# Two equal units a batch in the first stage of a fused attention and two-layer MLP kernel, and loads that gather across unit borders

## The chip, the cores and the metric

The kernel runs on one core of a Trainium2 chip. The metric is the device time of one launch in microseconds (us). Engines are named as in the profile: PE is the matrix engine (PEld its weight loads), DVE the vector engine, ACT the scalar engine, POOL GpSimd, SP the queue that issues every DMA of this kernel (SPq in the rows).

## What is computed

The reference, cut to what matters (B = 8 batches, H = 8 heads, S = 576 tokens, D = 64; 4608 tokens in all, d_model 512, d_ff 2048):

```
a = softmax(phi over 32 slots)
k_m, v_m = einsum('bhsm,bhsd->bhmd', a, k), the same with v
attn = softmax(q @ k_m^T / 8) @ v_m
x = attn, heads side by side: 4608 x 512
r = relu(x @ moe_w_in);  g = s * r * r + b
y = g @ moe_w_out
h = y @ moe2_w_in;  out = (h * sigmoid(1.702 h)) @ moe2_w_out
```

Every product of float32 matrices is made of three matmuls of a high part and a low part (fp32r): high by high, high by low, low by high.

## The kernel before

The program has four stages, one after the other on PE:

- **Stage 1** goes over the 8 batches of 576 tokens. For a batch, `slots` and `attend` make the attention weights of the tokens, 32 slots a head, transposed, and `weigh` leaves them as a high part `ah` and a low part `al` (two head groups, 576 columns each). `matrix` folds v_m into a quarter of moe_w_in on PE (tile `vw`), and ACT and DVE split that into `mh` and `ml`. `step` then makes 256 rows of `h = x @ moe_w_in` for one unit of tokens: 12 matmuls (2 row blocks, 2 head groups, 3 parts) whose moving operand is the unit's columns of `ah` or `al`. ACT (or DVE) takes relu of it into a tile `r`, and a DMA writes that to DRAM. A batch has 8 values of `pi` (256 rows each), and for each of these two units.
- **Stage 2** (`down("wo", "r", ...)`) goes over 6 spans of 768 tokens, each two half blocks of TS = 384 tokens. It loads `r` from DRAM as [128, 2, 384] tiles, five a span and quarter (A, B, C, D, E: 120 loads in all), squares them on ACT (line 642), combines and splits them on DVE and ACT (`ol`, `oh`) and makes seven products of a Strassen scheme; `leave` writes tiles `x`.
- **Stage 3** (`up`) reads `x` and writes `g`; **stage 4** (`down("w2", "g", ...)`) reads `g` and writes the output.

Since 576 is not a multiple of 384, the units of stage 1 are cut at the borders of the 384-token half blocks. `units(b)` yields them: 384 and 192 tokens for an even batch, 192 and 384 for an odd one. A unit of 384 tokens then fills one DRAM tile `r` of [128, 2 x 384] by itself; a unit of 192 tokens fills half of one, as 2 runs a partition of 192 values. `attend` and `weigh` make the attention columns in the same units; in batch 0 the two units are weighed one after the other, in the later batches together.

The order of the work is found at build time by `Order.sort`: each operation has a due time, a cost for each engine that can do it, and needs; the planner takes, engine by engine, what can start first, and writes the program in that order. `pe` costs a group of `count` matmuls of n columns as count x (n / 2.4 + 13.4) ns; `dma` and the loads cost kb / 340 us on SP. The due times of stage 1 go by B1 = 38.5 us a batch, and loads of stage 2 are due 14 to 16 us ahead of their product. Buffers come from pools of fixed numbers (`BUFS`): 31 of the tiles `t`, 4 of PSUM. In the start, until batch 0 is under way, PE runs filler matmuls of 128 columns (line 228) in front of a PSUM tile's first use.

The matmuls of `step` stand in the trace at lines 280 to 282 (helper `mm3`), their relu at line 598, the casts of every operand at line 258, the subtractions at line 264, stage 2's matmuls at lines 667 to 669, and every DMA at line 253.

Of the kernel before, what the change touches and what calls it, by code (L numbers as in the profile page):

```python
# [14 lines left out]
AF = mybir.ActivationFunctionType  # L15
ALU = mybir.AluOpType
# [136 lines left out]
class Net:  # L153
# [31 lines left out]
    B1, B2 = 38.5, 58.5  # L185
# [3 lines left out]
    def __init__(self, nc, tc, ctx, aps):  # L189
        self.nc, self.tc, self.a = nc, tc, aps  # L190
        self.B, self.S = aps["q"].shape[0], aps["q"].shape[3]
        self.sb = ctx.enter_context(tc.tile_pool(name="sb", bufs=1))
        self.ps = ctx.enter_context(tc.tile_pool(name="ps", bufs=1, space=PSUM))
        self.dr = ctx.enter_context(tc.tile_pool(name="dr", bufs=1, space=bass.MemoryType.DRAM))
        self.n = self.spare = 0
        self.T = {}
        self.order = Order(self.BUFS)
        self.d = {}
# [14 lines left out]

        return self.t(k, [P, 2, n], dt)

    def units(self, b):

        t = self.S * b
        while t < self.S * (b + 1):
            n = min(self.TS - t % self.TS, self.S * (b + 1) - t)  # L220
            m = t // self.TS
            yield t - self.S * b, n, m // 2, m % 2, t % self.TS
            t += n

    def pst(self, k):
# [261 lines left out]
    def attend(self, b, due, groups, apart):  # L487


        nc, T, S = self.nc, self.T, self.S  # L490
        at = [e[:2] for e in self.units(b)]
        qs = [("t", ("q", b, p)) for p in range(4)]
        kms = [("km", (b, g)) for g in range(2)]
        for p, k in enumerate(qs):
            self.dma(due - 8 + 0.5 * p, lambda k=k: self.t(k, [P, S]), lambda p=p: self.a["q"][b, p], (), (k,))
        for n, us in enumerate(groups):
            d = due + apart[1] * n
            ps = {u: ("ps", ("a", b, u)) for u in us}

            def score(us=us, ps=ps):  # L500
                for u in us:
                    out = self.pst(ps[u])
                    for p in range(4):
                        w = slice(32 * p, 32 * p + 32)
                        for g in range(2):
                            o = slice(64 * g, 64 * g + 64)
                            c, m = at[u]
                            nc.tensor.matmul(out[w, g, 0:m], T[kms[g]][o, w], T[qs[p]][o, c:c + m], start=True, stop=True)

            self.pe(d, 2200 * sum(at[u][1] for u in us) // S, score, (*qs, *kms), tuple(ps.values()))  # L510
            for g in range(2):
                self.weigh(b, g, us, [at[u] for u in us], ps, d, apart[0] * g)
# [65 lines left out]
        self.tt(due + 1, 1024, lambda: self.t(ml, [P, 2, 512], F32R), lambda: T[pm], lambda: T[mh].bitcast(F32), ALU.subtract, (pm, mh), (ml,))  # L578


    def step(self, b, pi, u, unit, due):
        nc, T = self.nc, self.T
        h, r = ("ps", ("h", b, pi, u)), ("t", ("r", b, pi, u))
        j = pi // 2
        c0, n, s, half, at = unit
        c = slice(c0, c0 + n)
        m = [("w", (x, b, j)) for x in ("mh", "ml")]
        ats = [[("t", (x, b, k)) for x in ("ah", "al")] for k in range(2)]

        def mm():  # L590
            out = self.pst(h)
            for i in range(2):
                o = slice((2 * pi + i) % 4 * P, (2 * pi + i) % 4 * P + P)
                self.mm3(out[:, i, 0:n], [([T[x][:, k, o] for x in m], [T[x][:, c] for x in ats[k]]) for k in range(2)])

        self.pe(due, n, mm, (*m, *((*x, u) for k in ats for x in k)), (h,), count=12)
        self.order.add(due + 0.5, [
            self.act(2 * n, lambda: nc.scalar.activation(self.two(r, n=n), T[h][:, :, 0:n], AF.Relu), psum=True),  # L598
            self.dve(2 * n, lambda: nc.vector.tensor_scalar(self.two(r, n=n), T[h][:, :, 0:n], 0.0, None, op0=ALU.max))], (h,), (r,))
        to = ("r", s, pi % 4, pi // 4, half)  # L600
        self.dma(due + 2, lambda: self.dram(*to).rearrange("p (a t) -> p a t", a=2)[:, :, at:at + n], lambda: T[r], (r,), ((*to, at),), n // 2)


    def operand(self, due, i, key, src, n):
# [10 lines left out]
        self.tt(due, 2 * self.TS, (lambda: self.two(out)) if new else (lambda: T[out]), lambda: T[a], lambda: T[b], ALU.subtract,  # L615
                [k for k in (a, b) if k != out], (out,))

    def load(self, due, k, name, *index):
        r = [x for x in self.order.wrote if x[:1 + len(index)] == (name, *index)]
        self.dma(due, lambda: self.two(k).rearrange("p a b -> p (a b)"), lambda: self.dram(name, *index), r, (k,), 384)  # L620

    def down(self, name, src, s, due):

# [107 lines left out]
    def up(self, s, due):  # L731

        nc, T, TS = self.nc, self.T, self.TS
        n = 2 * TS
        R = {(j, k): ("t", (f"x{j}{k}", s)) for j in range(2) for k in range(2)}
        for j, k in ((0, 0), (1, 0), (0, 1), (1, 1)):
            self.load(due - 26 + 2 * j + 4 * k, R[j, k], "x", s, j, k)
        r11, r12, r21, r22 = R[0, 0], R[0, 1], R[1, 0], R[1, 1]
        t2 = ("t", ("t2", s))
        op = {}  # L740
        d = due - 12
# [14 lines left out]
        for q in range(4):  # L756
            X, Y, Z = (("ps", (x, "w1", s, q)) for x in "XYZ")
            to = {1: X, 2: Z, 6: X, 7: Y, 5: X, 3: X, 4: Y}
            a, u2, u4 = (("t", (x, "w1", s, q)) for x in ("a", "u2", "u4"))
            for at, i in enumerate(seq):  # L760
                d = due + q * pair + at * pas
# [17 lines left out]
                e = d + pas  # L779
# [45 lines left out]
    def plan(self):  # L825
# [8 lines left out]
        for b in range(B):  # L834
            s0 = b * B1
            if b == 0:
                for g in range(2):
                    self.slots(0, g, -42 + 4 * g, 10)
                self.attend(0, -28, ((0,), (1,)), (2, 6))
            for j in range(4):  # L840
                if b == 0:
                    for c in range(4):
                        k = ("w", ("wi", j, c // 2))

                        def make(k=k, c=c):
                            if c % 2 == 0:
                                self.t(k, [P, 2, 512])
                            return self.T[k][:, c % 2]

                        self.convert(9.6 * j - 24 + 2 * c, (*k, c % 2), make, self.a["wi"][4 * j + c], 24 - 2 * c if j == 0 else 6)  # L850
                d = s0 + j * B1 / 4
                self.matrix(b, j, d - (24 if b == j == 0 else 8))
                if b == 0 and j == 2:
                    self.warm(d, False)
                for i in range(2):
                    for u, unit in enumerate(self.units(b)):
                        self.step(b, 2 * j + i, u, unit, d + B1 / 8 * (i + unit[0] / self.S))
                if b + 1 < B and j < 2:
                    self.slots(b + 1, j, s0 + 2 + 8 * j)
                elif b + 1 < B and j == 2:  # L860
                    self.attend(b + 1, s0 + 18, ((0, 1),), (4, 0))
            if b in (2, 3, 4, 6):
                q = (2, 3, 4, 6).index(b)
                self.prepare("wo", q, s0 + 2, keep=q == 3, step=3)
# [95 lines left out]
```

## Time and profile before

| | before |
|---|---|
| median of 3 runs | 1403.19 us (1402.94 to 1405.13) |
| the profiled execution's own time | 1407.16 us |
| its span in the profile | 1405.2 us |
| PE / DVE / ACT busy, share of the span | 98% / 74% / 57% |
| granted PE clock, mean | 0.995 |
| DMA moved | 347.74 MB, 247 GB/s over the span |

Busy time of PE counts a matmul from its start to its modelled end; successive matmuls overlap, so the distance from start to start, not the duration, is what one costs. In the rows, an entry such as "0.33 PE L281" is a duration, and the number at the row's start is the start time in us from the beginning of the span.

### The profile page before, as it was taken

The numbers are of one execution on the slowest core, as the hardware profiler recorded it, in microseconds if no ns is written. First come the engines' busy times: TensorE is split into PE (matmuls) and PEld (weight loads), VectorE is DVE, ScalarE is ACT, GpSimd is POOL, SyncE is SP. The second block draws the span as 40 slices with busy tenths as digits, with TensorE's granted clock in tenths as the row PEclk, the third lists the DMA queues.
The fourth block names the chain that finished last, engine by engine and source line by source line (L and its number), as shares of the span: only waits on it lengthen the run. The fifth ranks groups of instructions, "written<-read, shape, count | busy, mean of one in ns | idle before, by whom it ended". The sixth has DMA issues, their size and how long they took to land.

```text
span 1405.2 us, 23985 instructions
## 1 busy us (share of the span) xinstructions
PE 1381.0 (98%) x9250; PEld 1328.2 (95%) x9250; DVE 1041.4 (74%) x1411; ACT 795.8 (57%) x1113; POOL 92.0 (7%) x70
## 2 busy tenths in 40 slices
PE   7899999999999999999999999999999999999998
PEld 6788888789999999999999999999999999999998
DVE  6959898786698888988876756565356967869682
ACT  4456665576677787687745655554335434434341
POOL 1401110100100100000110110100000000000000
PEclk9999999999999999999999999999999999999999
DMA  9979999899875585499979674764896465344541
GB/s 349 305 255 302 378 368 332 291 311 358 280 246 187 182 277 173 153 320 320 337 261 345 259 271 166 257 238 147 277 360 242 155 195 177 125 158 162 195 138 45
DMA packets 134576, 347.74 MB, mean 247 GB/s; under 512 B 14400, under 2 KB 30784, under 8 KB 134464
## 3 DMA queue, kind: packets, MB, share of 16 engines
q1 hardware_dynamic: 134464, 346.24, 71.0%
q8 instruction: 72, 1.18, 0.3%
q14 instruction: 40, 0.33, 0.1%
HBM read 211.44 MB, written 134.74 MB: 246 GB/s over the span
## 4 chain that ended last, share of the span: by engine, by line
PE 85%; DMA 7%; DVE 6%; ACT 1%; issue 1%; SPq 1%; ACTq 0%; DVEq 0%
PE X L667 9%; PE X L669 9%; PE X L668 9%; PE Y L668 4%; PE Y L669 4%; PE Y L667 4%; PE X L774 4%; PE X L775 4%; PE X L776 4%; PE h L280 4%; PE h L282 4%; PE h L281 4%; PE Z L669 2%; PE Z L667 2%; PE Z L668 2%; DMA w<-w 2%
## 5 line engine op out<-in xcount | busy, mean ns | idle before, releaser
L282 PE MATMUL h<-ah,ml 128*128 128x384 f32 (+1 forms) x512 | 157.1, 307 | 5.5 <-DVE ml L264 5.5
L280 PE MATMUL h<-ah,mh 128*128 128x384 f32 (+1 forms) x512 | 161.0, 314 | 0.8 <-ACT km L258 0.5
L264 DVE TENSOR_TENSOR u<-Y,u 128x768 f32<-128x768 f32 x60 | 57.4, 956 | 135.5 <-ACT u L782 69.5
L281 PE MATMUL h<-al,mh 128*128 128x384 f32 (+1 forms) x512 | 156.6, 306 | 0.7 <-DVE al L264 0.7
L667 PE MATMUL X<-oh,wo 128*128 128x384 f32 x384 | 129.2, 337 | 2.9 <-ACT u L693 2.9
L774 PE MATMUL X<-oh,w 128*128 128x384 f32 x384 | 128.5, 335 | 1.1 <-ACT a L782 0.7
L668 PE MATMUL X<-ol,wo 128*128 128x384 f32 x384 | 129.0, 336 | 0.0
L669 PE MATMUL X<-oh,wo 128*128 128x384 f32 x384 | 128.8, 336 | 0.0
L776 PE MATMUL X<-oh,w 128*128 128x384 f32 x384 | 128.3, 334 | 0.0
L775 PE MATMUL X<-ol,w 128*128 128x384 f32 x384 | 128.3, 334 | 0.0
L667 PE MATMUL X<-oh,w 128*128 128x384 f32 x384 | 128.3, 334 | 0.0
L668 PE MATMUL X<-ol,w 128*128 128x384 f32 x384 | 128.3, 334 | 0.0
L669 PE MATMUL X<-oh,w 128*128 128x384 f32 x384 | 128.3, 334 | 0.0
L598 ACT ACTIVATE r<-h 128x768 f32<-128x768 f32 (+1 forms) x127 | 82.4, 651 | 67.6 <-PE h L282 54.9
L258 ACT CAST oh<-C 128x768 fp32r<-128x768 f32 x93 | 76.4, 835 | 67.2 <-PE X L669 26.0
L280 PEld LDWEIGHTS h<-ah,mh 128*128 128x128 f32 x512 | 97.8, 191 | 17.5 <-issue 6.3
L264 DVE TENSOR_TENSOR ol<-A,oh 128x768 fp32r<-128x768 f32 x96 | 91.9, 967 | 17.0 <-PE X L668 7.1
L282 PEld LDWEIGHTS h<-ah,ml 128*128 128x128 f32 x512 | 97.4, 190 | 6.6 <-DVE ml L264 6.6
L281 PEld LDWEIGHTS h<-al,mh 128*128 128x128 f32 x512 | 97.4, 190 | 1.6 <-DVE al L264 1.6
L264 DVE TENSOR_TENSOR ol<-C,oh 128x768 fp32r<-128x768 f32 x96 | 90.8, 956 | 8.1 <-ACT oh L258 4.0
L264 DVE TENSOR_TENSOR ol<-E,oh 128x768 fp32r<-128x768 f32 x48 | 45.8, 957 | 61.6 <-PE Y L668 21.4
L322 POOL TENSOR_TENSOR cw<-cw,raw 128x512 uint32<-128x512 uint32 x32 | 47.0, 1469 | 579.6 <-DVE cw L319 365.3
(192 smaller groups left out, 3725.7 us busy)
## 6 DMA issues: line engine op xcount, KB each, us to landing
w<-w SPq DMA_DIRECT2D x112, 512.0 KB, 5.6
r<-r SPq DMA_DIRECT2D x64, 384.0 KB, 5.2
wo<-wo SPq DMA_DIRECT2D x42, 512.0 KB, 6.0
g<-u SPq DMA_DIRECT2D x48, 384.0 KB, 3.2
kv<-in_kv SPq DMA_DIRECT2D x64, 258.0 KB, 5.3
raw<-in_w SPq DMA_DIRECT2D x32, 512.0 KB, 5.2
r<-r SPq DMA_DIRECT2D x64, 192.0 KB, 5.0
q<-in_q SPq DMA_DIRECT2D x32, 288.0 KB, 5.5
```

The source lines that it names most:

```text
L258: self.order.add(due, [self.act(n, lambda: nc.scalar.copy(out(), src()), psum), self.dve(n, lambda: nc.vector.tensor_copy(out(), src()), f ...
L264: self.order.add(due, [self.dve(n, lambda: nc.vector.tensor_tensor(out(), a(), b(), op=op), port=port)], r, w, first)
L280: self.nc.tensor.matmul(ps, wh, xh, start=start and i == 0, stop=False)
L281: self.nc.tensor.matmul(ps, wh, xl, start=False, stop=False)
L282: self.nc.tensor.matmul(ps, wl, xh, start=False, stop=(i == n - 1))
L598: self.act(2 * n, lambda: nc.scalar.activation(self.two(r, n=n), T[h][:, :, 0:n], AF.Relu), psum=True),
L667: nc.tensor.matmul(out, T[w][:, 0, c], T[h][:, p], start=f, stop=False, skip_group_check=True)
L668: nc.tensor.matmul(out, T[w][:, 0, c], T[l][:, p], start=False, stop=False, skip_group_check=True)
L669: nc.tensor.matmul(out, T[w][:, 1, c], T[h][:, p], start=False, stop=last, skip_group_check=True)
L774: nc.tensor.matmul(out, T[w][:, 0, c], T[h][:, k], start=f, stop=False, skip_group_check=True)
L775: nc.tensor.matmul(out, T[w][:, 0, c], T[l][:, k], start=False, stop=False, skip_group_check=True)
L776: nc.tensor.matmul(out, T[w][:, 1, c], T[h][:, k], start=False, stop=k == 1, skip_group_check=True)
```

## The change

Stage 1 works in two equal units of 288 tokens a batch (`HS = S // 2`), and the DRAM tiles of `r` are these units: one of [128, 2 x 288] for each batch, `pi` and unit, written by one DMA whose every partition is one run. `units` goes away; the new `pieces(m)` yields, for half block m of 384 tokens, the two units that it lies in, where in the unit and where in the tile, and how many tokens: 288 + 96, 192 + 192 or 96 + 288. `load` gathers an `r` tile of stage 2 by two DMAs from two DRAM tiles; loads of `x` and `g` stay one DMA each. `step` and `attend` take the fixed unit size; the due times of the two units are half a step apart, where they stood at 0 and two thirds, or 0 and a third.

```
+        self.HS = self.S // 2
-    def units(self, b):
-        t = self.S * b
-        while t < self.S * (b + 1):
-            n = min(self.TS - t % self.TS, self.S * (b + 1) - t)
-            m = t // self.TS
-            yield t - self.S * b, n, m // 2, m % 2, t % self.TS
+    def pieces(self, m):
+        t, end = self.TS * m, self.TS * (m + 1)
+        while t < end:
+            u, at = divmod(t, self.HS)
+            n = min(self.HS - at, end - t)
+            yield u // 2, u % 2, at, t - self.TS * m, n
             t += n
...
     def attend(self, b, due, groups, apart):
-        at = [e[:2] for e in self.units(b)]
+        at = [(0, self.HS), (self.HS, self.HS)]
...
-    def step(self, b, pi, u, unit, due):
+    def step(self, b, pi, u, due):
-        c0, n, s, half, at = unit
-        c = slice(c0, c0 + n)
+        c = slice(u * HS, u * HS + HS)
...
-        self.pe(due, n, mm, (*m, *((*x, u) for k in ats for x in k)), (h,), count=12)
+        self.pe(due, HS, mm, (*m, *((*x, u) for k in ats for x in k)), (h,), count=12)
...
-        to = ("r", s, pi % 4, pi // 4, half)
-        self.dma(due + 2, lambda: self.dram(*to).rearrange("p (a t) -> p a t", a=2)[:, :, at:at + n], lambda: T[r], (r,), ((*to, at),), n // 2)
+        to = ("r", b, pi % 4, pi // 4, u)
+        self.dma(due + 2, lambda: self.dram(*to, cols=2 * HS), lambda: T[r].rearrange("p a b -> p (a b)"), (r,), (to,))
...
-    def load(self, due, k, name, *index):
-        r = [x for x in self.order.wrote if x[:1 + len(index)] == (name, *index)]
-        self.dma(due, lambda: self.two(k).rearrange("p a b -> p (a b)"), lambda: self.dram(name, *index), r, (k,), 384)
+    def load(self, due, k, name, s, i, j, half):
+        if name != "r":
+            at = (name, s, i, j, half) if name == "g" else (name, s, j, half)
+            self.dma(due, lambda: self.two(k).rearrange("p a b -> p (a b)"), lambda: self.dram(*at), (at,), (k,), 384)
+            return
+        nc, HS = self.nc, self.HS
+        ps = [(("r", b, i, j, u), t, c, n) for b, u, t, c, n in self.pieces(2 * s + half)]
+        def go():
+            x = self.two(k)
+            for at, t, c, n in ps:
+                nc.sync.dma_start(x[:, :, c:c + n], self.dram(*at).rearrange("p (a t) -> p a t", a=2)[:, :, t:t + n])
+        self.order.add(due, [("sync", 384 / 340, go, False)], [p[0] for p in ps], (k,))
...
-                    for u, unit in enumerate(self.units(b)):
-                        self.step(b, 2 * j + i, u, unit, d + B1 / 8 * (i + unit[0] / self.S))
+                    for u in range(2):
+                        self.step(b, 2 * j + i, u, d + B1 / 16 * (2 * i + u))
```

Three places show what this does to the order of instructions (a row is line, operation, written tile, read tiles, size of what is written). The first is on PE in batch 1, just behind a `vw` product: the first unit's last two matmuls and the second unit's first one, before:

```order
L282 MATMUL h_1067<-ah_1031,ml_1029 128x192
L280 MATMUL h_1082<-ah_988,mh_958 128x384
L281 MATMUL h_1082<-al_990,mh_958 128x384
L282 MATMUL h_1082<-ah_988,ml_1029 128x384
L280 MATMUL h_1082<-ah_1031,mh_958 128x384
```

and with the change:

```order
L283 MATMUL h_1067<-ah_1031,ml_1029 128x288
L281 MATMUL h_1086<-ah_985,mh_958 128x288
L282 MATMUL h_1086<-al_1004,mh_958 128x288
L283 MATMUL h_1086<-ah_985,ml_1029 128x288
L281 MATMUL h_1086<-ah_1031,mh_958 128x288
```

The matmuls stand in the same order and number, and both units have 288 columns.

The second is on SP in stage 1, batch 0: the writes of `r` between the loads of the next batch, before:

```order
L253 DMA r_2_0_0_744<-r_693 128x768
L253 DMA kv_747<-in_kv 128x516
L253 DMA r_2_0_1_759<-r_711 256x1x192
L253 DMA ph_779<-in_phi 128x640
L253 DMA raw_785<-in_wo 128x1024
L253 DMA r_3_0_0_793<-r_742 128x768
```

and with the change:

```order
L254 DMA r_2_0_0_742<-r_693 128x576
L254 DMA kv_746<-in_kv 128x516
L254 DMA r_2_0_1_763<-r_710 128x576
L254 DMA ph_766<-in_phi 128x640
L254 DMA r_3_0_0_785<-r_744 128x576
L254 DMA kv_793<-in_kv 64x516
```

Of each pair of writes the second had 256 runs of 192 values; now both have 128 runs of 576.

The third is on SP at the start of stage 2, where its tiles are loaded, before:

```order
L253 DMA E_4794<-r_0_1_1_928 128x768
L253 DMA A_4799<-r_0_0_0_1142 128x768
L253 DMA wo_4818<-wo_1_2417 128x1024
L253 DMA E_4836<-r_1_1_1_986 128x768
L253 DMA A_4841<-r_1_0_0_1207 128x768
L253 DMA wo_4858<-wo_2_2971 128x1024
```

and with the change:

```order
L630 DMA E_4910<-r_0_1_1_930 128x2x192
L630 DMA E_4910<-r_0_1_0_1384 128x2x192
L630 DMA A_4914<-r_0_0_0_1122 128x2x96
L630 DMA A_4914<-r_0_0_1_1143 128x2x288
L630 DMA E_4934<-r_1_1_1_987 128x2x192
L630 DMA E_4934<-r_1_1_0_1469 128x2x192
```

Each load is two DMAs that stand side by side, with two runs a partition each, where it was one DMA with one run. Behind the last unit of stage 1, the rows of PE stand in the same order as before.

## Rows read from the trace of the kernel before

**Rows 1.** Windows: stretch, length, busy us by engine (instructions), clock, DMA share, GB/s

```profile
24.00:62.00 38.00, 33.06 (x331) 28.92 (x323) 36.87 (x78) 23.00 (x41) 10.91 (x9) 0.96 0.94 332
80.00:116.00 36.00, 36.00 (x374) 30.30 (x373) 21.20 (x37) 18.70 (x30) 1.31 (x1) 1.00 0.64 215
116.00:152.00 36.00, 35.34 (x350) 30.00 (x350) 34.15 (x57) 24.89 (x42) 4.71 (x3) 1.00 0.99 349
188.00:225.00 37.00, 36.65 (x370) 30.41 (x369) 35.70 (x62) 22.71 (x36) 5.70 (x4) 1.00 0.91 326
300.00:352.00 52.00, 52.00 (x389) 47.80 (x388) 37.10 (x49) 34.15 (x49) 0.00 (x0) 1.00 0.94 345
352.00:720.00 368.00, 364.86 (x2094) 363.90 (x2093) 318.86 (x392) 271.19 (x378) 30.90 (x20) 1.00 0.73 245
```

**Rows 2.** Waits of PE, 80 to 352 us: total, times, longest (us)

```profile
PE h L281 <- DVE al L264: 0.7, 3, 0.4
...
PE h L282 <- DVE ml L264: 0.3, 1, 0.3
```

**Rows 3.** Waits of PE, 24 to 80 us, the longest

```profile
PE h L282 <- DVE ml L264: 5.2, 3, 4.0
```

**Rows 4.** Timeline of PE in stage 1: start, duration, line, operands, columns

```profile
169.25 0.27 PE L281 MATMUL h<-al,mh 128*128 128x192 f32 x1
...
170.36 0.28 PE L282 MATMUL h<-ah,ml 128*128 128x192 f32 x1
...
170.88 0.33 PE L281 MATMUL h<-al,mh 128*128 128x384 f32 x1
...
172.61 0.34 PE L282 MATMUL h<-ah,ml 128*128 128x384 f32 x1
```

**Rows 5.** Timeline of PE in the start: fillers, then the first unit

```profile
25.86 6.07 PE L228 MATMUL h<-ident 128*128 128x128 f32 x52
31.69 0.43 PE L280 MATMUL h<-ah,mh 128*128 128x384 f32 x1
```

**Rows 6.** Groups by shape: one of the three matmul lines of stage 1

```profile
L280 PE MATMUL h<-ah,mh 128*128 128x384 f32 x256 | 88.5, 346 | 0.4 <-ACT mh L258 0.4
...
L280 PE MATMUL h<-ah,mh 128*128 128x192 f32 x256 | 72.5, 283 | 0.5 <-ACT km L258 0.5
```

**Rows 7.** Groups by shape: the relu on ACT

```profile
L598 ACT ACTIVATE r<-h 128x768 f32<-128x768 f32 x64 | 51.9, 810 | 39.2 <-PE h L282 32.6 <-issue 2.3 <-DMA r<-r 1.8
...
L598 ACT ACTIVATE r<-h 128x384 f32<-128x384 f32 x63 | 30.8, 489 | 28.3 <-PE h L282 22.3 <-DMA r<-r 3.2 <-issue 1.1
```

**Rows 8.** Timeline of SP in stage 1: two successive writes of r

```profile
260.33 0.33 SPq L253 DMA_DIRECT2D r<-r  x1
...
263.35 0.53 SPq L253 DMA_DIRECT2D r<-r  x1
```

**Rows 9.** Issues of one load of stage 2 on SP: ns min/median/max

```profile
L253 SPq DMA_DIRECT2D B<-r x24: 319/320/694, 308.2 to 634.4; - x24
```

**Rows 10.** DMA issues: count, KB each, median us from issue to landing

```profile
r<-r SPq DMA_DIRECT2D x64, 384.0 KB, 5.2
...
r<-r SPq DMA_DIRECT2D x64, 192.0 KB, 5.0
```

**Rows 11.** DMA packets, 80 to 352 us; queue: packets, MB, share of 16 engines

```profile
DMA packets 43918, 87.68 MB, mean 322 GB/s; under 512 B 4145, under 2 KB 18632, under 8 KB 43888
...
q1 hardware_dynamic: 43888, 87.27, 90.3%
```

**Rows 12.** DMA queue, 1140 to 1200 us (runs of 768 values alone)

```profile
q1 hardware_dynamic: 3456, 9.44, 48.5%
```

**Rows 13.** DMA queue, 360 to 720 us

```profile
q1 hardware_dynamic: 29094, 87.71, 71.7%
```

**Rows 14.** Waits, 360 to 720 us: ACT for loads of r, and PE

```profile
ACT E L642 <- DMA E<-r: 7.7, 4, 3.3
...
ACT B L642 <- DMA B<-r: 5.9, 6, 1.7
...
ACT C L642 <- DMA C<-r: 3.1, 4, 1.3
...
ACT D L642 <- DMA D<-r: 2.8, 4, 0.9
...
PE X L667 <- ACT u L693: 2.9, 1, 2.9
```

More of the change, by code (lines that the diff above doesn't have):

```diff
@@ L578, in matrix @@
         self.tt(due + 1, 1024, lambda: self.t(ml, [P, 2, 512], F32R), lambda: T[pm], lambda: T[mh].bitcast(F32), ALU.subtract, (pm, mh), (ml,))
-    def step(self, b, pi, u, unit, due):
-        nc, T = self.nc, self.T
+    def step(self, b, pi, u, due):
+        nc, T, HS = self.nc, self.T, self.HS
         h, r = ("ps", ("h", b, pi, u)), ("t", ("r", b, pi, u))
         j = pi // 2
-        c0, n, s, half, at = unit
-        c = slice(c0, c0 + n)
+        c = slice(u * HS, u * HS + HS)
         m = [("w", (x, b, j)) for x in ("mh", "ml")]
@@ L593, in mm @@
                 o = slice((2 * pi + i) % 4 * P, (2 * pi + i) % 4 * P + P)
-                self.mm3(out[:, i, 0:n], [([T[x][:, k, o] for x in m], [T[x][:, c] for x in ats[k]]) for k in range(2)])
-        self.pe(due, n, mm, (*m, *((*x, u) for k in ats for x in k)), (h,), count=12)
+                self.mm3(out[:, i, 0:HS], [([T[x][:, k, o] for x in m], [T[x][:, c] for x in ats[k]]) for k in range(2)])
+        self.pe(due, HS, mm, (*m, *((*x, u) for k in ats for x in k)), (h,), count=12)
         self.order.add(due + 0.5, [
-            self.act(2 * n, lambda: nc.scalar.activation(self.two(r, n=n), T[h][:, :, 0:n], AF.Relu), psum=True),
-            self.dve(2 * n, lambda: nc.vector.tensor_scalar(self.two(r, n=n), T[h][:, :, 0:n], 0.0, None, op0=ALU.max))], (h,), (r,))
-        to = ("r", s, pi % 4, pi // 4, half)
-        self.dma(due + 2, lambda: self.dram(*to).rearrange("p (a t) -> p a t", a=2)[:, :, at:at + n], lambda: T[r], (r,), ((*to, at),), n // 2)
+            self.act(2 * HS, lambda: nc.scalar.activation(self.two(r, n=HS), T[h][:, :, 0:HS], AF.Relu), psum=True),
+            self.dve(2 * HS, lambda: nc.vector.tensor_scalar(self.two(r, n=HS), T[h][:, :, 0:HS], 0.0, None, op0=ALU.max))], (h,), (r,))
+        to = ("r", b, pi % 4, pi // 4, u)
+        self.dma(due + 2, lambda: self.dram(*to, cols=2 * HS), lambda: T[r].rearrange("p a b -> p (a b)"), (r,), (to,))
     def operand(self, due, i, key, src, n):
@@ L736, in up @@
         for j, k in ((0, 0), (1, 0), (0, 1), (1, 1)):
-            self.load(due - 26 + 2 * j + 4 * k, R[j, k], "x", s, j, k)
+            self.load(due - 26 + 2 * j + 4 * k, R[j, k], "x", s, None, j, k)
         r11, r12, r21, r22 = R[0, 0], R[0, 1], R[1, 0], R[1, 1]
```

## The prediction

> **What bounds the kernel now.** I read the windows first, cut at about one batch each [rows 1]. In stage 1 PE is busy nearly throughout (36.00 of 36 us from 80 to 116, 52.00 of 52 from 300 to 352) and in stage 2 364.86 of 368. Busy time of PE alone proves little, since matmuls overlap, so I read next what PE waited for: from 80 to 352 us six kinds of wait, of which the first and last stand in [rows 2]; they sum to 2.8 us in 272. So from batch 1 on PE's own stream sets the time of stage 1. Before that it does not: between 24 and 80 us PE waited 5.2 us for `ml` [rows 3], in a stretch where DVE is busy 36.87 of 38 us [rows 1]. The reader should also see that in two later batches DVE (34.15 of 36, 35.70 of 37) and DMA (0.99, 0.91) stand just behind PE [rows 1].
>
> **What a matmul costs.** The distance of starts in the timeline, not the duration, is the price. Ten steps of 192 columns take 170.36 - 169.25 = 1.11 us, 111 ns each; ten of 384 take 172.61 - 170.88 = 1.73, 173 ns each [rows 4]. The granted clock is 1.00 there, the level of 2.4 GHz, so the columns alone are 80 and 160 ns: 384 columns pay 13 ns over, 192 pay 31. The fillers tell why: 52 records of 128 columns fill 31.69 - 25.86 = 5.83 us, 112 ns each [rows 5]. 128 and 192 columns cost the same; there is a floor near 111 ns that columns do not set, and 384 is above it. With 13 ns over the columns, the floor ends at (111 - 13) x 2.4 = 235 columns. 288 lies above it: 288 / 2.4 + 13 = 133 ns.
>
> The Trainium skill (TensorE: Matmul & The Clock Gate, Back-to-back issue gap) gives N / 2.4 + 2.5 ns for a matmul alone, 122.5 ns at 288 columns, and with that price the first term below would be 768 x (284 - 245) = 30 us in place of 13.8. The trace does not agree: at 384 columns the same formula gives 162.5 where the rows show 173, so the measured 13 ns stand in the sum.
>
> **The change part by part.**
>
> *The matmuls of stage 1.* Each of the three lines has 256 matmuls of 384 columns and 256 of 192 [rows 6]: 768 pairs. Each pair goes from 173 + 111 = 284 ns to 2 x 133 = 266. 768 x 18 ns = **13.8 us** less PE time, 1.7 us a batch. The columns are the same in sum; what goes is the floor under the short unit. Of these 13.8 not all reach the end:
>
> - Batch 0 is set by DVE (97% busy, and PE waits for it), whose work the change leaves alike. I give up its 1.7 us. The first unit's chain is shorter and the second's longer; I count that as nothing, since only the order of equal work moves.
> - Two batches have 1.85 and 1.3 us of DVE's time free [rows 1]. If they shrink by 1.7, DVE is at 99 to 100% and must sometimes be waited for. I give up half of their saving, 1.7 us together; the bounds are nothing lost (part of that work prepares weights, which later batches with more room can take: 21.20 of 36 in the batch before) and all 3.5 lost.
>
> *Relu.* 810 ns for 768 values a partition and 489 for 384 [rows 7], 1299 a pair; at 576 by the line between them, 2 x 650. Nothing.
>
> *The writes of r.* A write whose every partition is one run issues in 0.33 us on SP, one of 256 runs in 0.53 [rows 8]. 64 of the latter become the former: 13 us less of SP's time, and half as many packets in these. SP issues ahead of need, and landing is alike (5.2 and 5.0 us [rows 10]), so I count nothing.
>
> *The loads of r in stage 2.* 120 loads of 0.32 us [rows 9] become 240 of 256 runs each, at 0.53 by [rows 8]: 0.74 us more SP time for each load, 89 us in all, spread over 368. What SP holds back meanwhile are the loads behind. What hides it: a load is due 14 us or more ahead of its product. If that cover is gone, ACT waits; it does so today 18 times for E, B, C and D, 19.5 us in all, while PE waits for none of it: its one long wait is 2.9 us for a PSUM tile [rows 14]. So I take nothing; the upper end is those 18 waits passed on to PE at 0.74 us, 13 us.
>
> *The DMA engines in stage 2.* They are 71.7% busy over 360 us, 258 us of time, and moved 87.71 MB [rows 13]; the loads are 120 x 384 KB = 47 MB of that, so some 139 us. Do short runs cost more? From 80 to 352 us 18632 - 4145 = 14487 packets have between 512 B and 2 KB [rows 11], the 768-byte runs of `r`. That stretch spent 0.903 x 16 x 272 = 3930 us of engine time on 87.27 MB, 45 ns per 1000 B; a stretch with runs of 3072 B alone spent 0.485 x 16 x 60 = 466 us on 9.44 MB, 49 ns [rows 11, 12]. So 768-byte runs cost no more than their bytes. The new runs have 1152, 768 and, in 80 of the 240 pieces, 384 bytes; the last no row shows. Below: proportional, 0. Above: a run of 384 B costs as much as one of 768, 80 x 256 runs x 384 B x 45 ns per 1000 B / 16 = 22 us, to 280 of 360. In neither case is the queue full, so I take 0 on the path.
>
> Sum: 13.8 - 1.7 - 1.7 = **10.4 us** less. The profiled execution took 1407.16 us, 2.0 outside its span and 4.0 above the median; the same difference is taken from the median: 1403.2 - 10.4 = **1392.8 us**, 0.7% less.
>
> **The rivals.**
>
> *DVE and DMA take PE's place in stage 1.* For: DVE at 95 to 97% in three of the stretches, DMA at 349 GB/s and 0.99. Then the savings of five batches (0 to 4) are lost, and 13.8 - 5 x 1.7 = 5.2 us remain: 1398. Against: PE waited 2.8 us in 272, and the planner, which places DVE's work, already reckons a pair as if it took 3.2 us for its 24 matmuls, which is the new price and not the old (24 x 142 = 3.4).
>
> *The pair does not get cheaper.* If the cost went straight from 111 ns at 192 columns to 173 at 384, 288 would cost 142 and nothing would be saved: 1403. For: the trace has no matmul between. Against: 128 and 192 cost the same, so there is a bend.
>
> *The gathers fill the DMA queue, and it is slower.* If loads in four times as many runs take f times the engines' time, stage 2 needs 258 + 139 (f - 1) us. It is full at f = 1.73, and the gain is gone from f = 1.81 on. At f = 2 the loads are 37 us too long: 1403 + 37 - 10 = 1430; at 1.85, 1409. For: f of writes need not be that of reads, and no row shows a run of 384 B. Against: the 768-byte writes, f = 1 [rows 11, 12]. The Trainium skill (DMA: Bandwidth & Descriptors, Specifications) puts the smallest run for full rate at 512 B, below which the engine reads, changes and writes back; here only the runs of 384 B fall under that, and no row shows what such a run costs.
>
> **How the numbers follow.** The forecast has a chance of 0.64; its own bounds are 1389.4 (all 13.8 us) and about 1396 (DVE's 3.5 lost, and a few of the late loads). DVE or DMA as the bound: 0.18, 1396 to 1400. No cheaper pair, or all of it given back in stage 2: 0.09, 1400 to 1406. Full queue: 0.05, above 1406. Better than 1389: 0.04. The range that leaves out no more than two in ten: 1388.8 to 1399.5. A difference of 0.2%, 2.8 us, is about what a measurement of this kernel can tell from none. Faster by over that: 0.64 + 0.18 + 0.04 and a part of the third case, 0.87; within it 0.07; slower 0.06.
>
> **What would show it.** In the profile of the changed kernel: starts of the 288-column matmuls 133 ns apart (142 is the second rival); stage 1's last unit ending some 10 us earlier; DVE's share in the batches near 1 and the waits of PE for `al` and `ml` still a few us (more than 8 is the first rival); the DMA share of stage 2 between 0.72 and 0.78, and PE's waits there near 3 us (a share above 0.9, with PE waiting for `ol` behind loads, is the third). The prediction is wrong if stage 2 gets longer by more than 2 us, or if stage 1 keeps its length with PE's matmuls closer together.

## The result and the profile after

| | before | after |
|---|---|---|
| median | 1403.35 us (1402.94 to 1405.13, 4 runs) | 1390.46 us (1387.85 to 1391.91, 4 runs) |
| ratio of the medians, 95% interval | | 0.9904 [0.9886, 0.9921] |
| the profiled execution's own time and span | 1407.16, 1405.2 us | 1387.85, 1386.1 us |

The change makes the kernel 12.9 us faster, 0.96%; forecast were 10.4 us to 1392.8. The profiled executions differ by 19.3 us, since that of before lay 4 us above its median and that of after 2.6 below. The 12.9 is what has to be explained, and what differs by one or two us between two profiles is read with that in mind.

The first thing to look at is the price of a matmul, in the timeline of PE in stage 1 of the changed kernel:

```profile
163.16 0.29 PE L282 MATMUL h<-al,mh 128*128 128x288 f32 x1
...
164.47 0.29 PE L283 MATMUL h<-ah,ml 128*128 128x288 f32 x1
```

Ten steps take 164.47 - 163.16 = 1.31 us, 131 ns each, and the mean over the units from 80 to 340 us that hold no wait and no missing record (second start to twelfth) is 132.6; the 133 worked out from 192 and 384 columns [rows 4] holds. The groups by shape of the page have the new row of relu:

```profile
L598 ACT ACTIVATE r<-h 128x576 f32<-128x576 f32 x128 | 83.2, 650 | 55.0 <-PE h L283 48.2
```

Of each of the three lines 512 matmuls of 288 columns stand where 256 + 256 stood [rows 6], and the relu takes the 650 ns forecast. The windows, cut as before [rows 1] as far as they can be, with one that shows where DVE's work went, and stage 2 (columns as there):

```profile
116.00:152.00 36.00, 36.00 (x384) 30.46 (x382) 34.48 (x59) 26.05 (x44) 5.56 (x4) 1.00 0.99 347
...
264.00:300.00 36.00, 36.00 (x386) 30.48 (x386) 33.75 (x59) 27.00 (x42) 4.00 (x4) 1.00 1.00 344
...
340.00:710.00 370.00, 367.16 (x2103) 364.00 (x2102) 320.37 (x394) 269.78 (x375) 28.97 (x20) 1.00 0.78 251
```

From 116 to 152 us PE now starts 384 matmuls where it started 350, from 188 to 225 399 where it started 370, with DVE busy 0.3 and 0.2 us more. DVE was as full as before and PE did not wait for it, as the waits of PE show, from 80 to 340 us in full:

```profile
PE h L281 <- ACT ah L259: 0.7, 1, 0.7
PE h L282 <- DVE al L265: 0.4, 1, 0.4
PE h L283 <- DVE ml L265: 0.2, 1, 0.2
```

1.3 us in 260, where they were 2.8 in 272. In batch 0 it waits as long for `ml` as before [rows 3], and 1.0 us for `al` besides (in all 7.8 us from 24 to 80 us, where they were 7.4):

```profile
PE h L283 <- DVE ml L265: 5.1, 3, 3.6
PE h L282 <- DVE al L265: 1.0, 1, 1.0
```

**How much stage 1 gained** is read from marks that both programs have, the products `vw` (the 20 of five batches lie between the first and the second mark) and the last matmul of a unit. Before, in the timeline of PE:

```profile
97.73 0.66 PE L574 MATMUL vw<-wi,km 64*32 64x512 f32 x8
...
286.18 1.09 PE L574 MATMUL vw<-wi,km 64*32 64x512 f32 x16
...
352.02 0.33 PE L282 MATMUL h<-ah,ml 128*128 128x384 f32 x1
```

and after:

```profile
93.20 1.09 PE L575 MATMUL vw<-wi,km 64*32 64x512 f32 x16
...
271.37 1.09 PE L575 MATMUL vw<-wi,km 64*32 64x512 f32 x16
...
334.22 0.29 PE L283 MATMUL h<-ah,ml 128*128 128x288 f32 x1
```

Up to the first mark 4.5 us are won, over five batches 188.45 - 178.17 = 10.3, behind the second mark 65.84 - 62.85 = 3.0. The marks do not cut the work alike, though: one unit (12 matmuls, 12 x 132.6 ns = 1.6 us) has moved across the first mark. Before, 22 units stand ahead of it and 79 between the marks, after, 21 and 80; behind the second mark stand 27 in both. For equal work the gains are 2.9, 11.9 and 3.0 us. And some 1.5 of the 2.9 are clock: from 24 to 62 us the granted clock is 0.96 before [rows 1] and 1.00 after.

Stage 1 ends 17.8 us earlier, not some 10. By the medians the whole program gains 12.9, so some 5 must have been lost again behind it. These two profiles do not show that loss, since that of before has a stall of 2.9 us at the border of the stages [rows 14]; it is looked for below. Stage 2's waits of PE (340 to 710 us, the largest) and its queue (350 to 710 us):

```profile
PE X L680 <- DVE ol L265: 2.1, 4, 0.7
...
PE X L679 <- ACT u L705: 0.2, 1, 0.2
```

```profile
q1 hardware_dynamic: 71997, 89.13, 76.7%
```

Of the one wait of 2.9 us for `u` [rows 14] 0.2 are left, and four for `ol` have come. The queue is 76.7% busy against 71.7 [rows 13], within the 258 to 280 us of 360 that were given.

### The profile page after: what moved, and what is told of

Its sections match the earlier page's. It is cut to its first block, busy times and chain, and to the rows that moved or that the text cites. A ratio compares the mean times of both kernels' runs of the same rounds, so it can differ in the third digit from the quotient of the medians.

```text
span 1386.1 us, 24257 instructions
## 1 busy us (share of the span) xinstructions
PE 1363.2 (98%) x9250; PEld 1310.2 (95%) x9250; DVE 1038.5 (75%) x1408; ACT 796.7 (57%) x1116; POOL 89.2 (6%) x70
## 4 chain that ended last, share of the span: by engine, by line
PE 87%; DVE 7%; DMA 3%; issue 1%; ACT 1%; SPq 0%; DVEq 0%; ACTq 0%
PE X L680 9%; PE X L681 9%; PE X L679 9%; PE X L786 5%; PE X L787 5%; PE X L788 5%; PE Y L680 4%; PE Y L681 4%; PE Y L679 4%; PE h L281 4%; PE h L283 4%; PE h L282 4%; PE Y L786 2%; PE Y L787 2%; PE Y L788 2%; PE Z L680 2%
## 5 line engine op out<-in xcount | busy, mean ns | idle before, releaser
L281 PE MATMUL h<-ah,mh 128*128 128x288 f32 x512 | 156.0, 305 | 1.1 <-ACT ah L259 0.7
L283 PE MATMUL h<-ah,ml 128*128 128x288 f32 x512 | 151.3, 295 | 5.4 <-DVE ml L265 5.3
L282 PE MATMUL h<-al,mh 128*128 128x288 f32 x512 | 151.0, 295 | 1.5 <-DVE al L265 1.4
L598 ACT ACTIVATE r<-h 128x576 f32<-128x576 f32 x128 | 83.2, 650 | 55.0 <-PE h L283 48.2
L265 DVE TENSOR_TENSOR ol<-A,oh 128x768 fp32r<-128x768 f32 x96 | 90.7, 955 | 14.8 <-PE X L680 7.7
```

The costliest lines, as they stand in the source:

```text
L265: self.order.add(due, [self.dve(n, lambda: nc.vector.tensor_tensor(out(), a(), b(), op=op), port=port)], r, w, first)
L281: self.nc.tensor.matmul(ps, wh, xh, start=start and i == 0, stop=False)
L282: self.nc.tensor.matmul(ps, wh, xl, start=False, stop=False)
L283: self.nc.tensor.matmul(ps, wl, xh, start=False, stop=(i == n - 1))
L598: self.act(2 * HS, lambda: nc.scalar.activation(self.two(r, n=HS), T[h][:, :, 0:HS], AF.Relu), psum=True),
```

## The experiments

Twelve kernels were run, in three groups, each against the kernel before on the same chip. The theory by then: the floor under the short unit is the whole gain, and the gathers take some back through SP. Rivals: the gain comes from something else that the equal units bring (whole writes, the planner's order), or the gathers cost through the DMA engines.

### 1. Is there a floor under 192 columns?

Of the kernel before, the short unit's matmuls are made 232 columns wide, in the same order:

```
+        w = max(n, 232)
+        k0 = w - n if c0 else 0
+        c = slice(c0 - k0, c0 - k0 + w)
...
-                self.mm3(out[:, i, 0:n], ...)
+                self.mm3(out[:, i, 0:w], ...)
```

> The kernel before, with every 192-column matmul of stage 1 widened to 232 columns (40 neighbouring columns are computed too and not read); the order of instructions is unchanged. Theory (a floor near 111 ns below about 235 columns): starts of the widened matmuls stay 111 to 112 ns apart, the time stays within 1 us of the kernel before. Rival (cost grows with columns from 192 on, 111 + 40 x 62/192 ns = 124 ns): 768 x 13 ns = 10 us slower.

1402.66 us, 0.9993 [0.9981, 1.0005] of before. The 768 matmuls with 40 more columns each cost nothing that shows. The timeline of PE says why:

```profile
169.61 0.27 PE L281 MATMUL h<-al,mh 128*128 128x232 f32 x1
...
170.73 0.28 PE L282 MATMUL h<-ah,ml 128*128 128x232 f32 x1
```

Ten steps in 1.12 us, 112 ns each, the price of 128 and of 192 columns. The floor reaches to 232 columns at least, and the second rival of the prediction falls.

### 2. Two loads for one, and the rest of the change left out

Of the kernel before, each load of `r` is cut in two as in the change, from one DRAM tile:

```
+        cut = (288, 192, 96)[(2 * index[0] + index[3]) % 3]
...
+            for c in (slice(0, cut), slice(cut, 384)):
+                self.nc.sync.dma_start(x[:, :, c], src[:, :, c])
```

> The kernel before, with each load of r in stage 2 cut into the two DMAs of the change (288 + 96, 192 + 192 or 96 + 288 tokens); stage 1 and the order of all other instructions unchanged. Theory (the gathers are hidden): within 1.5 us of the kernel before, DMA share of stage 2 up from 0.72 to about 0.77, ACT waiting longer for loads, PE not. Rival (the late loads reach PE, 18 waits at 0.74 us): up to 13 us slower.

1411.22 us, 1.0057 [1.0037, 1.0076]: 7.6 us slower. So two loads for one are not free, though the prediction took them so. Its windows show one place, 480 to 600 us (this profile's execution took 1416.42 us, 5 above the median):

```profile
480.00:600.00 120.00, 116.85 (x660) 115.64 (x660) 100.71 (x124) 86.41 (x119) 7.36 (x4) 0.99 0.66 205
```

against before:

```profile
480.00:600.00 120.00, 120.00 (x694) 119.96 (x693) 105.07 (x130) 89.66 (x124) 8.66 (x5) 1.00 0.65 216
```

PE starts 34 matmuls fewer in this stretch, some 5.9 us at 173 ns, while the DMA share stays at 0.66. One wait can be followed through all engines. In the kernel before, SP issues a row of eight loads and two other DMAs thus (first and last load), and ACT squares the last of them without waiting:

```profile
507.65 0.32 SPq L253 DMA_DIRECT2D B<-r  x1
...
518.29 0.38 SPq L253 DMA_DIRECT2D D<-r  x1
...
523.63 0.83 ACT L642 ACTIVATE D<-D 128x768 f32<-128x768 f32 x1
```

With two DMAs a load:

```profile
509.82 1.19 SPq L629 DMA_DIRECT2D B<-r  x2
...
523.42 1.19 SPq L629 DMA_DIRECT2D D<-r  x2
...
530.11 0.85 ACT L653 ACTIVATE D<-D 128x768 f32<-128x768 f32 x1 [1.68 <-DMA D<-r]
...
534.37 0.44 PE L678 MATMUL X<-oh,wo 128*128 128x384 f32 x1 [1.69 <-ACT oh L258]
```

The row takes SP 524.61 - 509.82 = 14.8 us, 13.3 of them issuing, in place of 11.0; its last load lands late, ACT waits 1.68 us for it, and PE 1.69 us for the cast behind that. Behind the wait the granted clock falls: it is 0.91 from 520 to 540 us, 1.8 us of the 5.9.

### 3. The same pieces on the writing side

The change's equal units, but `r` stays in DRAM as half blocks: a unit is written in one or two pieces, and a load is one DMA again. The planner's order changes with the number of DMAs.

```
+        for s, half, at, k0, n in self.pieces(b, u):
+            to = ("r", s, pi % 4, pi // 4, half)
+            self.dma(..., lambda ...: self.dram(*to)...[:, :, at:at + n], lambda ...: T[r][:, :, k0:k0 + n], ...)
```

> The change's equal units on PE, but r in DRAM by half blocks of 384 tokens as before: the units are written in pieces in stage 1, and each load of stage 2 is one DMA again. Theory (the gain is PE's matmuls in stage 1, wherever the pieces are cut): 11 to 14 us faster than the kernel before, 1389.5 to 1392.5. Rival (the whole-run writes of r in a stage with a DMA share near 1 make part of the gain): with 170 writes of short runs in place of 128 of whole ones, DMA and SP time in stage 1 grows and at least 4 us of the gain are lost.

1394.32 us, 0.9934 [0.9914, 0.9954]: 3.9 us slower than the change by the medians (the intervals overlap by 0.0007). Stage 1 ends at 339.2 us in place of 334.2. There its queue (80 to 340 us) is

```profile
q1 hardware_dynamic: 67068, 86.74, 98.6%
```

against the change's

```profile
q1 hardware_dynamic: 41689, 87.66, 95.0%
```

Here the pieces fall in the stage whose queue is already full; that this and not the new order costs the time is not shown. The cut has to be made somewhere, since 288 does not divide 384, and on the reading side it costs no more, by the medians less.

### 4. Where the cost of the gathers lies: four loads, and none

Of the change, each load of `r` goes in four DMAs of 96 tokens, all of 384-byte runs:

```
+                for o in range(0, n, 96):
+                    nc.sync.dma_start(x[:, :, c + o:c + o + 96], ...[:, :, t + o:t + o + 96])
```

> The changed kernel with every load of r in four DMAs of 96 tokens, all runs of 384 bytes (480 DMAs in place of 240); nothing else differs. Theory (a short run costs its bytes and little more, and stage 2 has DMA and SP time to spare): under 4 us slower than the changed kernel, 1390 to 1394, DMA share of stage 2 up to 0.85. Rival (a run under 512 bytes takes about double, f = 2): stage 2 needs 258 + 139 us of DMA in 360, and the kernel is 15 to 35 us slower than the changed one.

1500.82 us, 1.0685 [1.0659, 1.0711]: 110 us slower than the change, far outside what the theory and its rival gave. Its waits of PE from 340 to 800 us, the largest:

```profile
PE X L680 <- ACT u L706: 32.0, 7, 8.5
PE X L680 <- ACT oh L259: 26.0, 7, 8.5
```

its queue from 400 to 800 us:

```profile
q1 hardware_dynamic: 112983, 75.36, 67.3%
```

and SP, with its own longest wait, in a stretch in which PE waits 8.5 us for `u`:

```profile
SPq L254 <- POOL cw L323: 7.9, 1, 7.9
...
504.78 2.48 SPq L631 DMA_DIRECT2D E<-r  x4
507.37 2.52 SPq L631 DMA_DIRECT2D A<-r  x4
```

A load takes SP 2.5 us, four times 0.62. Not all of the 8.5 us is issuing: just before, SP stood 7.9 us at a DMA that waited for POOL (tile `cw`), and the loads of `r` stood behind it in SP's order. From 400 to 800 us SP issues for 266 us, so the mean share of the engines does not tell what limits the loads. A stretch in which SP issues with hardly a pause does, 72 issues from 355 to 404 us:

```profile
355.00:404.00 49.00, 37.54 (x203) 36.01 (x201) 27.39 (x38) 26.10 (x37) 2.99 (x3) 0.93 0.74 199
```

The DMA engines are 74% busy there. In such stretches it is the issuing that limits the loads, not the engines.

Then the change with the gather left out, one DMA of one run a load. The two units of a batch share one DRAM tile, and stage 2 works on other tokens of `r` than it should; the order on PE is the same.

```
+        self.dma(due + 2, lambda: self.dram(*to[:4], cols=4 * HS)[:, 2 * HS * u:2 * HS * (u + 1)], ...)
...
-            for at, t, c, n in ps:
-                nc.sync.dma_start(x[:, :, c:c + n], ...[:, :, t:t + n])
+            nc.sync.dma_start(self.two(k).rearrange("p a b -> p (a b)"), self.dram("r", b, i, j)[:, o:o + 768])
```

> The changed kernel, but each load of r in stage 2 is one DMA of one run of 768 values a partition, taken from one batch's tile (so the gather is left out and stage 2 works on other tokens of r); the order on PE, DVE, ACT and POOL is unchanged. Theory after the first four runs (the gathers do cost PE time in stage 2, by SP's 2 x 0.6 us a load, and the equal units give more than their sum): 5 to 8 us faster than the changed kernel, 1383 to 1386. Rival (the gathers cost something only beside the old units): within 1.5 us of the changed kernel, 1389 to 1392.

1385.52 us, 0.9876 [0.9860, 0.9891]: 4.9 us faster than the change, 17.9 us below before (1403.47 in this group). The change itself was timed in another group, so this difference goes by medians, and the two intervals overlap by 0.0005. It prices the gathers at 4.9 us in this program, and the rest of the change at some 18. Its waits of PE from 340 to 710 us, in full:

```profile
PE X L681 <- DVE ol L265: 0.4, 1, 0.4
PE Y L681 <- DVE ol L265: 0.2, 1, 0.2
```

They are 0.6 us against 2.7 in the change. The busy times show more of the difference, since a matmul counts as busy up to its modelled end, beyond the start of the next:

```profile
340.00:710.00 370.00, 369.32 (x2128) 368.40 (x2127) 323.74 (x399) 272.38 (x380) 30.43 (x20) 1.00 0.73 254
```

PE starts 2128 matmuls where the change started 2103: 25 fewer at 173 ns are 4.3 us, in stage 2, at a granted clock of 1.00 in both.

### 5. Two loads of half as many runs

The change with the two row blocks of `r` interleaved value by value in the tile, so that a piece is one run a partition; relu writes and stage 2's casts read with a stride of two.

```
+    def swap(self, x):
+        return x.rearrange("p a b -> p (a b)").rearrange("p (t a) -> p a t", a=2)
...
+                nc.sync.dma_start(x.rearrange("p a b -> p (a b)")[:, 2 * c:2 * (c + n)], self.dram(*at)[:, 2 * t:2 * (t + n)])
```

> The changed kernel with the two row blocks of r interleaved value by value, so that each piece of a load is one run a partition (128 runs a DMA in place of 256, same bytes, same 240 DMAs); relu writes and the casts and subtractions of stage 2 read with a step of two values. Order of instructions unchanged. Theory (SP's issue time by runs is what the gathers cost): issues fall from 0.6 to about 0.33 us and 3 to 6 us of the time come back, 1384.5 to 1387.5. Rival (it is the number of DMAs, or their landing, that costs): no gain. If reads at a step of two are slower on ACT or DVE, it is slower than the changed kernel.

1387.14 us, 0.9886 [0.9871, 0.9901]: 3.3 us of the 4.9 come back by the medians (the intervals overlap by 0.0015). The issues of one tile's loads on SP (ns, minimum, median and maximum), in the change:

```profile
L630 SPq DMA_DIRECT2D C<-r x48: 517/596/1427, 356.2 to 645.8; - x48
```

interleaved:

```profile
L635 SPq DMA_DIRECT2D C<-r x48: 319/382/1491, 357.3 to 644.6; - x48
```

and without the gather:

```profile
L631 SPq DMA_DIRECT2D C<-r x24: 319/320/404, 354.7 to 641.9; - x24
```

A load of this tile keeps SP 2 x 0.60 = 1.19, 2 x 0.38 = 0.76 and 0.32 us, and the times are 4.9, 1.6 and 0 us over the last. The interleaved pieces have half as many runs, but also longer ones, and that eases the engines too. From 342 to 366 us, where loads stand in a row, the change, interleaved, and without the gather:

```profile
342.00:366.00 24.00, 24.00 (x140) 24.00 (x140) 18.94 (x27) 16.77 (x25) 4.92 (x3) 1.00 1.01 320
342.00:366.00 24.00, 24.00 (x140) 24.00 (x139) 20.25 (x28) 16.35 (x24) 5.97 (x4) 1.00 0.98 348
342.00:366.00 24.00, 24.00 (x140) 24.00 (x140) 19.86 (x28) 16.84 (x24) 5.08 (x4) 1.00 0.97 349
```

The engines are full in all three, and move 320 GB/s with the gathers against 348 and 349. That the issuing alone can hold loads up is shown by experiment 4; how the 4.9 us divide between SP's issues and full engines no run separates.

### 6. Are the loads merely late?

The change, with the loads of `r` due 8 us earlier:

```
-                self.load(d - 14 - 2 * (x == 1), ...)
+                self.load(d - 14 - 2 * (x == 1) - 8 * (name == "wo"), ...)
```

> The changed kernel with the loads of r in stage 2 due 8 us earlier. Theory (loads come late because SP is busy with others just ahead of the need): 2 to 5 us faster than the changed kernel. Rival (a load waits for a free tile, not for its turn): no gain, within 1.5 us, or slower where tiles are held longer.

1395.26 us, 0.9948 [0.9933, 0.9963]: 4.8 us slower than the change. The waits of PE from 340 to 710 us, the larger of two:

```profile
PE X L680 <- DVE ol L265: 4.3, 7, 1.3
```

The same kind of wait, and more of it (for `ol` in all 6.6 us against 2.3). Due times also set how the planner ranks everything else and when buffers are taken, so this does not say which of these it was; only that an earlier due time is no cure.

### 7. What else could carry the extra gain

The rest of the change is worth some 18 us, and the matmuls by the sum only 13.8. Two candidates were tried on the kernel before. Whole writes: the 192-token units written as one run a partition (the values then stand in another order in the tile, and stage 2 works on permuted `r`).

```
-        self.dma(due + 2, lambda: self.dram(*to).rearrange("p (a t) -> p a t", a=2)[:, :, at:at + n], lambda: T[r], ...)
+        self.dma(due + 2, lambda: self.dram(*to)[:, 2 * at:2 * (at + n)], lambda: T[r].rearrange("p a b -> p (a b)"), ...)
```

> The kernel before, but each 192-token unit of r is written as one run of 384 values a partition (128 runs in place of 256; the values then stand in another order within the tile, so stage 2 works on permuted r); the order of instructions is unchanged. Theory (the equal units gain 13.8 us on PE and the writes in whole runs the rest of the 18 us that the change shows without its gathers): 3 to 5 us faster than the kernel before, about 1399. Rival (the rest comes from the planner's order): within 1.5 us of the kernel before.

1402.84 us, 0.9992 [0.9984, 1.0001]: at most some 2 us, and by the median 0.9. And the planner told the floor, so that its order goes by the true cost:

```
-        t = count * (n / 2.4 + 13.4) if count else self.COL * n
+        t = count * max(n / 2.4 + 13.4, 111.5) if count else self.COL * n
```

> The kernel before with the planner's cost of a matmul floored at 111.5 ns, so that it reckons the 192-column units at what they take; units, writes and loads unchanged, only the order differs. Theory (part of the rest of 4 us is small waits of an order made with too cheap short units): 2 to 4 us faster than the kernel before. Rival (writes, above): within 1.5 us.

1405.26 us, 1.0018 [1.0004, 1.0032]: slower, by 1.5 us over before in the same group. Neither carries the extra gain by itself.

### 8. Units of 256 and 320 tokens

Both above the floor, and the same 576 columns:

```
-        self.HS = self.S // 2
+        self.UN = ((0, 256), (256, 320))
```

> The change with units of 256 and 320 tokens in place of 288 and 288 (both above 235 columns). Theory (being above the floor counts, not being equal): starts 120 and 146 to 147 ns apart, a pair at the same 266 ns, and within 2 us of the changed kernel, 1388.5 to 1392.5. Rival (the equal length itself helps: buffers, eviction, order): 3 us or more slower than the changed kernel.

1394.25 us, 0.9931 [0.9918, 0.9944]: 3.8 us slower than the change by the medians (the intervals overlap by 0.0003). In the timeline of PE nine steps of 320 columns take 1.32 us, 147 ns each, and those of 256 columns 120, so a pair costs 267 ns, as with 2 x 133. What is lost is not on the matmuls' account. The waits of PE are 3.6 us against 1.3 in stage 1 (80 to 340 us), and in stage 2 (340 to 715 us) 3.2 for `ol` against 2.3 and 1.4 for `u` and `oh` against 0.4. Length is not all: with units of equal price but other lengths, and so another order, the small waits shift by a few us. Which of the two it is, length or order, is open.

### 9. Batch 0, and the best version

The wait of 3.6 us for the first `ml` is DVE's choice of order. In the change, `ml` of batch 0 is ranked ahead on DVE:

```
-        self.tt(due + 1, 1024, ..., ALU.subtract, (pm, mh), (ml,))
+        self.tt(due + 1, 1024, ..., ALU.subtract, (pm, mh), (ml,), 40 * (b == j == 0))
```

> The changed kernel with the first `ml` of batch 0 ranked ahead on DVE, so that it stands before the weights of the second unit; the rest of the order is almost the same. Theory (PE's wait of 3.6 us for it in the start, and a lower granted clock behind such a wait, are lost time): 1.5 to 3 us faster than the changed kernel. Rival (batch 0 is set by DVE's whole work): no gain.

1388.43 us, 0.9896 [0.9883, 0.9908]: 2.0 us faster than the change by the medians, with intervals that overlap. From 24 to 80 us PE waits 2.0 us for `al` and 1.4 for `ml`, 3.4 us in place of 6.1. This with the interleaved `r` of experiment 5:

> The changed kernel with r interleaved (one run a piece) and the first `ml` ranked ahead. Theory (the two are gains in different stages and add): 1385 us, 5 us faster than the changed kernel. Rival (a wait saved in the start returns as another in batch 1): 1387, no better than the interleaved one alone.

1385.44 us, 0.9877 [0.9863, 0.9891]: 5.0 us less than the change, where 3.3 + 2.0 = 5.3 were to be had, and 1.2% below before. It computes all that the reference does, and is the fastest version found.

## Why the prediction was right, and where it was not

The time fell where it was put, with the right mechanism for the gain, but in part by luck: the matmuls were taken 2.3 us too low and the losses to DVE too high, the gathers 4.9 us too low, and these errors nearly cancel.

**The matmuls, 13.8 us: the right price, a little too small a sum.** 131 to 134 ns were measured at 288 columns, and the bend at 235 columns worked out from three prices is borne out by 232 columns at 112 ns and 256 at 120. But the term multiplies a difference of rounded prices, each read off one unit. The means over the units from 80 to 340 us, taken as above, are 174.5 ns at 384 columns, 111.7 at 192 and 132.6 at 288: a pair falls by 174.5 + 111.7 - 2 x 132.6 = 21.0 ns, not 18, and 768 pairs by 16.1 us. The formula that the Trainium skill gives for a matmul alone (TensorE: Matmul & The Clock Gate, Back-to-back issue gap), by which the term would have been 30 us, gives 122.5 ns at 288 columns and does not agree; the runs decide for 13 ns over the columns above a floor of 111 to 112.

**The 3.4 us given up: "1.7 for batch 0" about right, "half of their saving" for two DVE-heavy batches mis-sized.** To compare at the same granted clock (0.96 from 24 to 62 us in both), the profile of experiment 1 is taken for before, which costs the same and lies at its kernel's median, and the one without the gathers for after, whose stage 1 is the change's:

```profile
97.61 1.09 PE L574 MATMUL vw<-wi,km 64*32 64x512 f32 x16
...
286.71 1.09 PE L574 MATMUL vw<-wi,km 64*32 64x512 f32 x16
```

```profile
94.62 1.09 PE L575 MATMUL vw<-wi,km 64*32 64x512 f32 x16
...
272.76 1.09 PE L575 MATMUL vw<-wi,km 64*32 64x512 f32 x16
```

Up to the first mark 3.0 us are won, 1.4 without the unit that moved; 21 to 22 units at 21.0 ns a pair would give 2.7. So some 1.3 us were lost in batch 0 and the start of batch 1. Between the marks 189.10 - 178.14 = 11.0 us are won, 12.6 with that unit, more than the 10.0 that its 79 to 80 units give at 21.0 ns: nothing was lost there, and the waits of PE fell besides (from 3.2 to 1.3 us). DVE had room in other batches, as the lower bound had it: from 80 to 116 us it is busy 23.25 us where it was 21.20 [rows 1], and from 264 to 300 us 33.75 where it was 31.68:

```profile
264.00:300.00 36.00, 35.34 (x360) 28.91 (x359) 31.68 (x54) 24.16 (x39) 4.59 (x3) 1.00 0.80 266
```

**The gathers, 0 us: wrong, 4.9.** The prediction laid the bounds at 0 and 13 us, "so I take nothing". The mechanism named for the upper end is the one that was found, loads held back behind SP and passed on to PE, as experiment 2 follows it; the issue cost was a little more than taken (0.60 in place of 0.53 us). What failed is the reading of the cover: it was judged by a mean, 89 us over 368, and by PE's present waits. But loads come in bursts. In the row of experiment 2 SP issued for 13.3 of 14.8 us, and what stood last came late. In such bursts the DMA engines are full as well and move less with the short runs (320 GB/s against 349 in experiment 5), which the prediction asked only of the mean share of the stage; how much of the 4.9 us is theirs stays open. The total stands on the runs with none, two and four issues a load (0, 4.9 and 115.3 us).

**The extra gain, not in the sum.** Without the gathers 17.9 us are won against 13.8. Of the 4.1, 2.3 are the rounding of the prices (16.1 - 13.8), and 1.5 the waits of PE from batch 1 on, which fell from 2.8 to 1.3 us. What is left is less than two profiles differ by: the loss in batch 0, and a us won behind stage 1 (1048.5 us in the profile of experiment 1, 1047.5 without the gathers). The wait of 2.9 us for `u` at the border of the stages [rows 14] is 0.2 in the profile of the change; but that wait differs between executions of one order of the matmuls (1.0 us in the profile of experiment 1, none in that of whole writes), so it can't be booked in full. Why the small waits fell is not shown; whole writes and a true cost for the planner do not bring it alone.

**The criterion.** "Wrong if stage 2 gets longer by more than 2 us": what follows the last matmul of stage 1 took 1386.1 - 334.2 = 1051.9 us after and 1405.2 - 352.0 = 1053.2 before, but before's profile has the stall at the border; in the profile of experiment 1, which lies at its kernel's median and runs the same stages, it was 1401.0 - 352.5 = 1048.5. So the condition came true by 3.4 us, and the forecast held since stage 1 gave more than was asked.

**The rivals.** DVE and DMA did not take PE's place: PE waits less than before with DVE at 95 to 97% and DMA at 0.99 to 1.02. The queue did not fill over the stage; what 384-byte runs cost the engines shows in experiment 4, where all loads of `r` are of these: 0.673 x 16 x 400 us for 75.36 MB is 57 ns per 1000 B, against 45 and 49 [rows 11, 12]. About half of these bytes are in runs of 384 B (102736 packets under 512 B), so by an estimate from these rows such a run costs 1.3 to 1.5 times its bytes' time. The Trainium skill (DMA: Bandwidth & Descriptors, Specifications) warns of runs under 512 B; the runs agree that those of 384 B cost more, and f stays below 1.81. (The prediction's 139 us counts all 120 loads into the 360 us of [rows 13]; 106 lie in them, so it is about 123, and the bound 1.83.)

## What to carry to other kernels

Cut a matrix product so that no unit lies below the floor of the issue rate: here 192 columns cost as much as 232. When a load is split, count the time that its issue takes on its queue over the burst in which it stands, not over the stage, and count it by runs; if pieces are needed, lay the data out so that each piece is one run a partition, and look at how full the DMA engines are where the pieces stand. Read the prices of a term that multiplies a small difference over many units, not off one. An engine that is 97% busy does not eat a saving if some of its work can slide into a later, lighter stretch.

## What the runs showed of the hardware

- **An issue on SP costs by its runs.** 128 runs take 0.32 us (0.38 in the median of an interleaved tile), 256 from 0.53 [rows 8] to 0.62, at lengths from 384 B to 1152 B. Four DMAs of 256 runs a load kept SP at 2.5 us a load and, while it issued with hardly a pause, the DMA engines at 74%.
- **A float32 operand with a stride of two costs ACT 8 to 9%, DVE nothing.** In the best version ACT casts operands of stage 2 with values two apart in 899 ns, against 830 in the change, and writes relu so in 707 against 650; DVE's subtraction takes 955 against 953 (`C`, 340 to 690 us). The row:

```profile
L263 ACT CAST oh<-C 128x768 fp32r<-128x768 f32 x46 | 40.7, 899 | 10.2 <-PE X L686 5.0 <-DMA x<-u 2.3 <-DVE C L269 1.3
```

- **The granted clock after a wait of PE is not the same each time.** Behind the wait of 2.9 us at the border the profile of before shows 0.66, a mixture of 2.4 and 1.2 GHz:

```profile
371.00:376.00 5.00, 4.10 (x15) 4.10 (x16) 1.21 (x3) 4.07 (x7) 1.90 (x1) 0.66 1.03 400
```

Behind the wait of 3.6 us for the first `ml`, the change shows 1.00 and the change without gathers, whose stage 1 is the same, 0.73, in the same window:

```profile
36.00:42.00 6.00, 4.99 (x39) 4.56 (x38) 5.81 (x12) 4.29 (x8) 1.41 (x1) 1.00 1.04 359
```

```profile
36.00:42.00 6.00, 6.00 (x39) 6.00 (x38) 5.79 (x13) 4.43 (x9) 1.42 (x1) 0.73 0.99 317
```

Such a drop costs about 1.7 us (5 us x 0.34), a share of what two single executions differ by.
